# A transfer of turned attention weights issued by ScalarE's queue in place of SP's, in every second round

## The chip, the core and the metric

The kernel runs on one core of a Trainium2 chip. Its engines are TensorE (PE in the profile, with PEld for the loading of matrix weights), VectorE (DVE), ScalarE (ACT), GpSimd (POOL) and SyncE (SP). Each works through its own list of instructions in order and waits on semaphores for the others. A DMA is issued by an instruction in such a list: SP's list holds little else, and ScalarE can issue DMAs too, between its computations. The metric is the device time of one launch in microseconds (us), the median of several runs.

## What is computed

The reference is an attention block with a threshold, followed by a two-layer network. All of it is float32.

```python
# q, k, v: (8, 8, 576, 64) = batch, heads, sequence, head size
scores = scale * np.matmul(q, k.transpose(0, 1, 3, 2))
thresh = np.max(scores, axis=-1, keepdims=True) - tau
scores = np.where(scores >= thresh, scores, -1000000000.0)
scores = scores - np.max(scores, axis=-1, keepdims=True)
attn = np.exp(scores)
attn = attn / (np.sum(attn, axis=-1, keepdims=True) + 1e-09)
out = np.matmul(attn, v)
# bridge: (B,H,S,D) -> (B*S, H*D), so x is (4608, 512)
h = x @ w_in                      # (512, 2048)
g = np.where(h > 0.0, h, np.exp(np.minimum(h, 0.0)) - 1.0)
y = g @ w_out                     # (2048, 512)
```

## The kernel before

**Pairs, steps and rounds.** Two heads of one sequence make a pair; there are 32 (`NP`). The 576 queries of a pair are taken in five steps: steps 0 to 3 have 128 queries of each head, and the tail step, which the code calls `NC` (4), has the last 64 queries of both heads. Pairs 0 to 8 are worked in an opening phase whose order is written out as a long list. From pair 9 (`START`) on there is a loop over rounds `pr` = 9 to 33. A round has the scores of its pair, the turned weights and values of earlier pairs, and 28 quarters of the network's matrix products, which are worked with a fast matrix scheme of seven products (the functions `first_product` and `second_round`, whose matmuls are recorded under line 825).

**One round on TensorE.** First come the scores of steps 0 and 1 (`wide_step(pr, 0)`, line 867), then the scores of the tail step together with the values of pair `pr - 2` (`tail_step`, lines 963, 966 and 974), then 14 quarters, then the scores of steps 2 and 3 (`wide_step(pr, 1)`, line 867 again) and 14 more quarters. A round takes about 33.5 us.

**Scores.** `wide_scores` writes the scores of two steps and two heads, four blocks of 576 columns, into one PSUM tile of six banks of 512 columns each, in eight pieces. After the piece that begins head 1's block of the second step, ScalarE copies one column of it into a small tile called `seen` (line 870). The function `on_banks` keeps a list of the accesses to each PSUM bank and makes an instruction wait for other engines' accesses to its banks. The blocks lie thus that `seen` reads column 1216, and the last piece of the call for steps 2 and 3 writes columns 1024 to 1216. VectorE then takes the row maxima (line 874), ScalarE the exponentials (887), VectorE the mask with the sums (891), and the weights are divided by their sums.

**Turning.** The values need the attention weights transposed. VectorE transposes them in squares of 32 (`turn_squares`, lines 695 and 708); four DMAs then send the squares to a place in DRAM called `there` (line 729, or line 714 for the tail step), and one DMA fetches them back with the squares in their right places (`fetch`, line 740; line 744, with two DMAs, for the tail step). What is fetched lands in the tiles `wTa` (steps 0 and 1) and `wTb` (steps 2 and 3 and the tail). From round 9 on the tail step's transposed squares of pair `pr` are first written to the place in `wTb` that step 3 of pair `pr - 1` will be fetched into, and the sends of line 714 read them there. Round `pr` fetches all five parts of pair `pr - 1`, and round `pr + 1` uses them at line 963.

**The order around the fetch.** The order of every engine's instructions is fixed when the kernel is built. A clock of estimated times runs along TensorE's work; an agenda holds the other engines' work under due times, each with an offset from tables (`MOVED`, keyed `f` for odd rounds and `s` for even ones, and `FIRST` for single rounds); what is due by then is emitted before the next piece of TensorE's work. The five fetches of a round have the due times 9.0, 12.5, 16.0, 20.0 and 24.0 us into it. For the last of them, step 3's, the table has

```python
"ffetch3": -5.52, ... "sfetch3": -3.76,
```

and in odd rounds step 2's fetch has +0.22, so step 3's comes first there. The costs that the clock adds in a round are 2.15 for a wide step, 1.2 + 2.2 + 1.8 for the tail step and 0.87 for each quarter (`QT`).

**SP's queue.** Before the change SP issues everything in the rounds: the sends and fetches of turned weights, the loads of q, k and v (lines 380, 394, 396), of sums of the network's weights (`sw`, line 1168, and `t`, line 1196), and the stores. ScalarE issues three DMAs at the start of the kernel and four stores at its end. Each DMA tells of its landing on a semaphore; these semaphores are few and are used in turn, over both queues, in the order in which the DMAs were emitted.

Of the kernel before, what the change touches and what calls it, by code (L numbers as in the profile page):

```python
# [216 lines left out]
def kernel(  # L217
# [10 lines left out]
    nc = tc.nc  # L228
# [139 lines left out]
    def load(pr, parts=("qm", "km", "v"), shared=False, queue=nc.sync, pieces=tuple((i, d) for i in range(2) for d in range(2)),  # L368
             js=slice(0, S // T)):
        b, j = divmod(pr, NPAIR)  # L370
        tiles = raws.setdefault(pr, {})
        for name, src in (("qm", q), ("km", k)):
            if name not in parts:
                continue
            if name not in tiles:
                tiles[name] = raw.tile([P, S // T, T], FP32, name="qm" if shared else name)
            m = tiles[name]
            for i, d in pieces:
                r = (2 * i + d) * T
                queue.dma_start(  # L380
                    m[r : r + T, js],
                    src[b, 2 * j + i].rearrange("(j t) d -> t j d", t=T)[:, js, d * T : (d + 1) * T],
                )
        if "v" in parts:
            load_v(pr, queue)
# [226 lines left out]
    def turned_tile(pr, i):  # L612
        part = int(i >= 2)
        if pr < NPAIR and i < 2:
            if (pr, "block", i) not in wTs:
                wide_one = (pr + i * NPAIR) % 2
                wTs[pr, "block", i] = wtp.tile([P, (2 + wide_one) * NT, NCH, T], FP32, name="wTb" if wide_one else "wTa")[:, :NT]
            return wTs[pr, "block", i], 0
        if (pr, part) not in wTs:
            wide_one = part  # L620
            wTs[pr, part] = wtp.tile([P, (2 + bool(wide_one)) * NT, NCH, T], FP32, name="wTb" if wide_one else "wTa")[:, : (2 + part) * NT]
        return wTs[pr, part], i % 2 * NT + (NT // 2 if part else 0)
# [112 lines left out]
    def fetch(pr, i, queue=nc.sync):  # L735
        back = turns.pop((pr, i)).rearrange("c k p n -> (c k) p n")
        fetched.add((pr, i))
        wT, g0 = turned_tile(pr, i)
        if i < NC:
            queue.dma_start(wT[:, g0 : g0 + NT].rearrange("p g c n -> p g (c n)"), back)  # L740
        elif pr >= JOINED:
            for h in range(2):
                g = h * (3 * NT - 2)
                queue.dma_start(
                    wT[:, g : g + 2, h * NC : h * NC + NC + 1].rearrange("p g c n -> p g (c n)"),
                    back[:, 2 * h : 2 * h + 2],
                )
        else:
            queue.dma_start(
                wT.rearrange("p (a b) c n -> p a b (c n)", b=2)[:, ::5],  # L750
                back.rearrange("k (a b) n -> k a b n", b=2),
            )
# [453 lines left out]
    def half_sums_x(g, rooms, j, engine=nc.vector):  # L1206
        (b11, b12), (b21, b22) = ([xts[g][:, k + j, t : t + CT] for t in (0, CT)] for k in (0, 2))
        xs = [x[:, j] for x in rooms]
        tt = engine.tensor_tensor
        return [lambda: tt(xs[0], b11, b22, ALU.add), lambda: tt(xs[1], b11, b12, ALU.add), lambda: tt(b12, b12, b22, ALU.subtract),  # L1210
                lambda: tt(xs[2], b21, b22, ALU.add), lambda: tt(b21, b21, b11, ALU.subtract)]
# [341 lines left out]
    with tc.manual_schedule():  # L1553
# [8 lines left out]
        def at(t, f, key=None):  # L1562
            if key and stage[0]:
                t += MOVED.get(stage[0] + key, 0.0)
                t += FIRST.get(f"{stage[3]}:{key}", 0.0)
            elif key:
                t += FIRST.get(f"e:{key}", 0.0)
            serial[0] += 1
            heapq.heappush(agenda, (t, serial[0], f))
# [244 lines left out]
        def group(g):  # L1814
            for r in range(2):
                for u in range(RU * r, RU * r + RU):
                    queue.append((first_product, (g, u)))
                queue.append((second_round, (g, r)))
# [66 lines left out]
        def wide_step(pr, half):  # L1885
            while pr > START and not {("q", pr), ("k", pr)} <= prepared:
                do_next()
            t = clock[0]
            on_pe(2.15, lambda: wide_scores(pr, half, seen_too=not half))
            e = t + 2.15  # L1890
            for s in range(2):
                i = 2 * half + s
                at(e + BOUNDS[half][s], lambda i=i: wide_bounds(pr, i), f"bound{i}")
                for h in range(2):
                    when = PLANS[half][s, h]
                    at(e + when[0], lambda i=i, h=h: wide_max(pr, i, h), f"max{i}{h}")
                    at(e + when[1], lambda i=i, h=h: wide_exp(pr, i, h), f"exp{i}{h}")
                    at(e + when[2], lambda i=i, h=h: wide_mask(pr, i, h), f"mask{i}{h}")
                finish_of(pr, i, e + SUMS[half][s], e + TURNS[half][s])
# [55 lines left out]
        for pr in range(START, NP + 2):  # L1955
            t = clock[0]
            b = pr // NPAIR
            stage[:] = "sf"[pr % 2], 0, 0, pr
            if pr == START + 1:
                ges.append((raw.tile([P, S // T, T], FP32, name="km").rearrange("p j d -> p (j d)")[:, : 2 * CT], lambda: None))  # L1960
            if pr == START:
                for x in range(3):
                    at(t + 18.0 + 6.0 * x, lambda x=x: nc.sync.dma_start(wout_sums[0, x], out_sums[x].rearrange("p u n -> p (u n)")))
            if pr <= NP:
                for i, when in ((NC, 9.0), (0, 12.5), (1, 16.0), (2, 20.0), (3, 24.0)):
                    at(t + when, lambda pr=pr, i=i: fetch(pr - 1, i), f"fetch{i}")
            if pr < NP:
                at(t + 9.0, lambda pr=pr: load(pr, ("v",)))
            if pr < NP:
                wide_step(pr, 0)  # L1970
            tail_step(pr)
            v_end = clock[0]
            if pr % NPAIR == 0 and pr > START:
                in_sums["x", b - 1] = [late["x"].tile([P, 2, CT], FP32, name=f"x{x}") for x in range(3)]
                jobs = half_sums_x(b - 1, in_sums["x", b - 1], 0)
                for x, when in ((1, 5.0), (0, 6.0), (2, 11.0), (3, 15.0), (4, 17.0)):
                    at(v_end + when, jobs[x], f"xsum{x}")
            if pr % NPAIR == 1:
                if b > 1:
                    if ("x", b - 1) in in_sums:  # L1980
                        jobs = half_sums_x(b - 1, in_sums["x", b - 1], 1)
                        for x, when in ((1, -5.0), (0, -0.6), (2, 0.1), (3, 0.5), (4, 1.0)):
                            at(v_end + when, jobs[x], f"ysum{x}")
                    else:
                        jobs = sums_x(b - 1, [late["x"].tile([P, 2, CT], FP32, name=f"x{x}") for x in range(3)])
                        for x, when in ((1, -3.0), (0, -0.6), (2, 0.3), (3, 1.0), (4, 1.8)):
                            at(v_end + when, jobs[x], f"xsum{x}")
                if pr < NP + 1:
                    group(b - 1)
            if pr == NP + 1:  # L1990
                break
            extras(t + 0.6, t + 2.8, t + 6.0, t + 8.0, t + 11.0, t + 14.0, t + 17.0)
            next_q(pr)
            ffn_quarters(HALF_QUARTERS)
            if pr < NP:
                e = clock[0] + 2.15
                wide_step(pr, 1)
                next_k(pr)
                extras(e + 0.3, e + 1.2, e + 4.2, e + 10.4, e + 12.0)
                ffn_quarters(HALF_QUARTERS)  # L2000
            else:
                extras(clock[0] + 0.6)
                ffn_quarters(5)
                while not all((NP - 1, i) in turns_done for i in range(NB)):
                    do_next()
                for r in range(2):
                    for m in DEEP:
                        if PRODUCTS[m][1][0] == "w" and (r, m) not in WHOLE:
                            weigh(r, m)
                for x in range(14):  # L2010
                    at(clock[0] + 0.56 * x + 0.1, lambda: bundles.popleft()(), f"w{x}")
                ffn_quarters(HALF_QUARTERS - 5)
# [332 lines left out]
```

## Time and profile before

| | |
|---|---|
| median of 3 runs | 1247.09 us (1246.99 to 1248.81) |
| the profiled execution | 1250.28 us |
| its span, first to last instruction | 1248.5 us |
| TensorE busy | 1232.1 us, 99% |
| VectorE busy | 1065.3 us, 85% |
| GpSimd busy | 800.9 us, 64% |
| ScalarE busy | 582.5 us, 47% |
| DMA queue of SP (q1) | 275.57 MB, 79.3% of 16 engines' span |
| DMA queue of ScalarE (q10) | 0.69 MB, 0.2% |
| issues of step 2's and 3's fetches (wTb at line 740) | 58, median 6.5 us to landing |

How the rows are read: a timeline row has the start in us from the span's start, the duration in us, the engine, the line of the kernel, the operation, the tile written and the tile read, and how many instructions the row takes together; in brackets stands the engine's idle time before it and what ended it. A `q` behind the engine's name marks its queue: the instruction issues or waits, and is not counted as busy. A row of waits has who waited for whom, then the sum in us, the number of times and the longest. The chain of waits through the profiled execution is on TensorE for 76% of the span.

### The profile page before, as it was taken

The page shows a single profiled execution, that of the slowest core. Times are in us where ns is not written, and L with a number is a line of the kernel's source. Part 1 is how long each engine was busy: PE and PEld are TensorE (multiplying, and loading weights), DVE is VectorE, ACT ScalarE, POOL GpSimd, SP SyncE. Part 2 cuts the span into 40 slices and gives each one's busy share as a digit, 9 for nine tenths or more (in the row PEclk, how much of TensorE's full clock was granted, in tenths as well). Part 3 has the DMA queues.
Part 4 walks back from the last instruction along what each step waited for, and adds up shares of the span by engine and source line. Part 5 has one row for each costly group of instructions (what it writes and reads, how often), then busy time and mean ns, then how long its engine had stood idle before and what let it go on. Part 6 is the DMA issues. An engine that isn't in the chain of part 4 may idle for free.

```text
span 1248.5 us, 32325 instructions
## 1 busy us (share of the span) xinstructions
PE 1232.1 (99%) x12020; PEld 832.1 (67%) x12020; DVE 1065.3 (85%) x2357; ACT 582.5 (47%) x1295; POOL 800.9 (64%) x1151
## 2 busy tenths in 40 slices
PE   8999999999999999999999999999999999999998
PEld 6776575566666666666666666666666666678887
DVE  6998989888899889988898889988998886777877
ACT  7987755453534445353525353444535350434130
POOL 5776644786576848583867657675858383675564
PEclk9999999999999999999999999999999999999999
DMA  9568999899989889898989888898889876444433
GB/s 222 150 185 243 235 251 269 240 275 243 247 215 273 225 259 222 251 252 243 243 231 262 226 267 219 245 238 252 220 257 251 233 223 231 165 136 153 140 110 118
DMA packets 332942, 278.33 MB, mean 223 GB/s; under 512 B 201328, under 2 KB 288368, under 8 KB 332784
## 3 DMA queue, kind: packets, MB, share of 16 engines
q1 hardware_dynamic: 331264, 275.57, 79.3%
q8 instruction: 95, 1.56, 0.5%
q10 hardware_dynamic: 1520, 0.69, 0.2%
q14 instruction: 63, 0.52, 0.1%
HBM read 178.85 MB, written 97.32 MB: 221 GB/s over the span
## 4 chain that ended last, share of the span: by engine, by line
PE 76%; DVE 4%; DMA 3%; SPq 1%; issue 1%; ACT 1%; POOL 1%; DVEq 0%; ACTq 0%
PE f L825 45%; PE sc L825 13%; PE sc L867 7%; PE f L974 7%; PE f L963 1%; DMA there<-x 1%; DVE mx L874 1%; DVE x L695 1%; PE sc L974 1%; DMA wTb<-there 1%; DVE e L891 1%; DVE w_one L891 0%; SPq L380 0%; DMA qm<-in_k_dram 0%; DMA wTa<-there 0%
## 5 line engine op out<-in xcount | busy, mean ns | idle before, releaser
L874 DVE TENSOR_REDUCE mx<-sc 128x1 f32<-128x576 f32 x252 | 180.2, 745 | 13.3 <-PE sc L867 4.8
L887 ACT ACTIVATE w_one<-sc,mx 128x576 f32<-128x576 f32 x140 | 102.9, 741 | 111.1 <-DVE wTb L708 44.3
L883 POOL TENSOR_SCALAR th<-mx,ntau 128x2 f32<-128x2 f32 (+1 forms) x139 | 56.9, 411 | 150.7 <-DVE mx L874 144.6
L891 DVE SCALAR_TENSOR_TENSOR w_one<-sc,th,w_one 128x576 f32<-128x576 f32 x140 | 111.4, 810 | 23.9 <-POOL e L544 9.9
L867 PE MATMUL sc<-kT,qT 64*64 64x320 f32 (+5 forms) x1792 | 121.6, 409 | 1.7 <-DVE w_one L891 1.7
L887 ACT ACTIVATE e<-sc,mx 128x576 f32<-128x576 f32 x112 | 82.3, 745 | 69.6 <-DVE mx L874 64.4
L544 POOL TENSOR_SCALAR w_one<-w_one,rs 128x576 f32<-128x576 f32 x115 | 92.7, 812 | 30.1 <-DVE rs L601 30.1
L867 PEld LDWEIGHTS sc<-kT,qT 64*64 64x64 f32 x1792 | 79.3, 132 | 47.5 <-issue 15.2
L825 PE MATMUL f<-w_out_sb,s 128*64 128x256 f32 (+1 forms) x896 | 105.6, 376 | 0.0
L825 PE MATMUL f<-x,w_in_sb 128*64 128x256 f32 x832 | 101.0, 379 | 0.0
L891 DVE SCALAR_TENSOR_TENSOR e<-sc,th,e 128x576 f32<-128x576 f32 x112 | 87.5, 807 | 8.1 <-ACT e L887 6.9
L825 PE MATMUL f<-t,s 128*64 128x256 f32 (+1 forms) x800 | 93.5, 375 | 0.0
L825 PE MATMUL f<-xt,sw 128*64 128x256 f32 x736 | 91.2, 381 | 1.1 <-DVE g L1638 0.6
L825 PE MATMUL f<-xt,w_in_sb 128*64 128x256 f32 x736 | 90.5, 379 | 0.0
L695 DVE STREAM_TRANSPOSE x<-e 128x640 f32<-128x640 f32 x108 | 77.5, 756 | 14.5 <-POOL e L544 12.4
L544 POOL TENSOR_SCALAR e<-e,rs 128x576 f32<-128x576 f32 x92 | 68.2, 748 | 31.3 <-DVE rs L601 30.0
L695 DVE STREAM_TRANSPOSE x<-w_one 128x512 f32<-128x512 f32 (+1 forms) x117 | 83.3, 749 | 5.6 <-DMA there<-x 2.6
L825 PEld LDWEIGHTS f<-w_out_sb,s 128*64 128x64 f32 x896 | 63.7, 137 | 31.5 <-issue 3.2
L870 ACT COPY seen<-sc 128x1 f32<-128x1 f32 x79 | 12.6, 159 | 154.0 <-PE sc L867 154.0
L825 PEld LDWEIGHTS f<-x,w_in_sb 128*64 128x64 f32 x832 | 61.5, 137 | 28.4 <-ACT g L1677 0.3
L825 PEld LDWEIGHTS f<-t,s 128*64 128x64 f32 x800 | 57.1, 137 | 28.0
L1703 POOL TENSOR_TENSOR s<-g 128x256 f32<-128x256 f32 x96 | 71.0, 742 | 1.9 <-DVE g L1666 1.9
(392 smaller groups left out, 3006.7 us busy)
## 6 DMA issues: line engine op xcount, KB each, us to landing
there<-x SPq DMA_DIRECT2D x452, 144.0 KB, 3.8
wTb<-there SPq DMA_DIRECT2D x58, 576.0 KB, 6.5
wTa<-there SPq DMA_DIRECT2D x55, 576.0 KB, 5.2
sw<-win_sums SPq DMA_DIRECT2D x62, 384.0 KB, 4.9
t<-wout_sums SPq DMA_DIRECT2D x45, 512.0 KB, 4.8
wTb<-there SPq DMA_DIRECT2D x56, 160.0 KB, 2.8
wst<-in_moe_w_in_dram SPq DMA_DIRECT2D x16, 512.0 KB, 4.3
vm<-in_v_dram SPq DMA_DIRECT2D x64, 128.0 KB, 2.8
```

Source lines behind the costliest of these rows:

```text
L544: nc.gpsimd.tensor_scalar(wv, wv, st["rs"][:, h : h + 1], 1.0, ALU.mult, ALU.mult)
L695: nc.vector.transpose(x[:, :, c0 : c0 + nc_], src.rearrange("p (c g n) -> p g c n", c=nc_, n=T))
L825: (note or beside)(nc.tensor.matmul(oy, left[:, y : y + D] if n > D else left, right, skip_group_check=True, **how), oy)
L867: on_banks(nc.tensor.matmul(oy, qT[r, i * P + y * D : i * P + (y + 1) * D], kT[r, k0 : k0 + n], start=True, stop=True, skip_group_check=Tr ...
L870: on_banks(nc.scalar.copy(seen, o[:, :1]), o[:, :1], kept=False)
L874: on_banks(nc.vector.tensor_reduce(st["mx"][:, h : h + 1], st["sc", h], axis=AX.XY if len(st["sc", h].shape) > 2 else AX.X, op=ALU.max, ne ...
L883: nc.gpsimd.tensor_scalar(st["th"][:, cs], st["mx"][:, cs], -1.0, ntau, ALU.mult, ALU.add)
L887: on_banks(nc.scalar.activation(st["e", h], st["sc", h], AF.Exp, bias=st["mx"][:, h : h + 1]), st["sc", h])
L891: on_banks(nc.vector.scalar_tensor_tensor(st["e", h], st["sc", h], st["th"][:, h : h + 1], st["e", h], ALU.is_ge, ALU.mult, accum_out=st[" ...
L963: watch(nc.tensor.matmul(o, vd[r, r], parts[x][r, g0:g1, NC], start=True, stop=False, skip_group_check=True), o)
L974: watch(nc.tensor.matmul(o, vm[:, h, c], parts[part][:, g0:g1, h * (NC + 1) + c], start=False, stop=(c == NC - 1), skip_group_check=True), o)
L1703: engine.tensor_tensor(o, x, y, op)
```

## The change

In the rounds `pr` = 9, 11, ..., 31 the fetch of step 3 of pair `pr - 1` is issued by ScalarE, on its own DMA queue; in the even rounds, and for the other four parts, SP issues as before. The due time, and with it the place of the fetch in the order in which the kernel emits its instructions, stays. The transfer, its source and its destination stay.

```diff
             if pr <= NP:
                 for i, when in ((NC, 9.0), (0, 12.5), (1, 16.0), (2, 20.0), (3, 24.0)):
-                    at(t + when, lambda pr=pr, i=i: fetch(pr - 1, i), f"fetch{i}")
+                    at(t + when, lambda pr=pr, i=i: fetch(pr - 1, i, nc.scalar if i == 3 and pr % 2 else nc.sync), f"fetch{i}")
```

`fetch` had the parameter for the queue already; in the opening phase it is called with it as well.

## The prediction

> **What bounds the kernel now.** I read the page's table of busy time, then the list of TensorE's waits, then the timelines of SP, ScalarE and TensorE around one of the fetches that move.
>
> ```profile
> span 1248.5 us, 32325 instructions
> PE 1232.1 (99%) x12020; PEld 832.1 (67%) x12020; DVE 1065.3 (85%) x2357; ACT 582.5 (47%) x1295; POOL 800.9 (64%) x1151
> PEclk9999999999999999999999999999999999999999
> ```
> ```profile
> PE f L963 <- DMA wTb<-there: 1.2, 1, 1.2
> ...
> PE f L963 <- issue: 0.6, 1, 0.6
> ...
> PE f L963 <- DVE g L1666: 0.4, 1, 0.4
> ```
>
> TensorE is the bound: 1232.1 of 1248.5 us, at the full granted clock. A gain must come out of its few waits, and a pause forced on it is added whole, for nothing else can run in its place. The three waits quoted stand at the start of rounds 18, 22 and 26, where line 963 needs the turned weights of the round before: 2.2 us in all. So no other transfer of turned weights is late, and nothing here can give back more than about 2 us.
>
> **The change part by part.** It hits rounds 9, 11, ... 31, twelve issues. I take round 15, whose fetch of the fourth step is the issue at 472.87. SP's timeline:
>
> ```profile
> 461.97 1.82 SPq L714 DMA_DIRECT2D there<-wTb  x4
> 463.83 0.43 SPq L740 DMA_DIRECT2D wTa<-there  x1
> 464.31 2.39 SPq L380 DMA_DIRECT2D qm<-in_k_dram  x4
> 466.79 2.68 SPq L1168 DMA_DIRECT2D sw<-win_sums  x1
> 469.57 3.25 SPq L729 DMA_DIRECT2D there<-x  x4
> 472.87 0.44 SPq L740 DMA_DIRECT2D wTb<-there  x1
> ```
>
> ScalarE's in the same stretch:
>
> ```profile
> 466.04 0.37 ACT L1678 COPY g<-f 128x256 f32<-128x256 f32 x1 [0.49 <-PE f L825]
> 468.70 0.16 ACT L870 COPY seen<-sc 128x1 f32<-128x1 f32 x1 [2.29 <-PE sc L867]
> ...
> 470.94 0.37 ACT L1630 COPY w<-f 128x256 f32<-128x256 f32 x1 [0.36 <-PE f L825]
> ```
>
> *Where it stands on ScalarE.* By the agenda the fetch is emitted 18.48 us into an odd round (24.0 with the -5.52 of its table entry); the second wide step comes at 2.15 + 5.2 + 14 x 0.87 = 19.53. So on ScalarE's queue the issue stands after the copy of line 1678 (done at 466.41) and ahead of the small copy into seen (468.70). ScalarE would meet it 2.3 us before seen is due, and 4 us before SP, which is in arrears here, gets to it (472.87).
>
> *What it will wait for.* The older DMAs show that an issue waits for another landing than those of its data:
>
> ```profile
> 436.25 1.24 SPq L740 DMA_DIRECT2D wTb<-there  x2
> 437.53 2.55 SPq L729 DMA_DIRECT2D there<-x  x4
> 440.12 5.67 SPq L380 DMA_DIRECT2D qm<-in_q_dram  x4
> ```
> ```profile
> SPq L380 <- DMA wTb<-there: 2.7, 2, 1.5
> ```
>
> The third and fourth load of line 380, which share no tile with the two fetches, waited 2.7 us for these to land. Each stands eight issues behind the fetch it waited for (fetch, fetch, four sends, two loads, load). Completion semaphores are taken in turn, eight of them, and an issue waits until the DMA eight before it has landed; the records of ScalarE's four issues at the very end use the same eight. In round 15 the eight before the fetch are four sends, one load of sums and three loads of k, so it hangs on the second load of line 380:
>
> ```profile
> 464.79 0.50 SPq L380 DMA_DIRECT2D qm<-in_k_dram  x1
> DMA to landing us min/median/max: 5.5/5.5/5.5
> ```
>
> That lands at 464.79 + 5.5 = 470.29, which is 1.59 us after seen now starts. On SP this costs nothing: SP comes to the fetch at 472.87. ScalarE would sit in front of it.
>
> *Who waits behind it.* Behind the issue stand seen, the exponentials and the copies out of PSUM. The nearest is seen. It reads column 1216 of the wide PSUM tile; the last piece of the same scores (192 columns) writes columns 1024 to 1216; both lie in one bank of 512, and the code makes TensorE wait for the other engines' accesses to a bank. TensorE's rows:
>
> ```profile
> 467.65 2.17 PE L867 MATMUL sc<-kT,qT 64*64 64x448 f32 x32
> ```
> ```profile
> 469.32 0.51 PE L867 MATMUL sc<-kT,qT 64*64 64x192 f32 x6
> ```
> ```profile
> L867 PEld LDWEIGHTS sc<-kT,qT 64*64 64x64 f32 x1792 | 79.3, 132 | 47.5 <-issue 15.2
> ```
>
> Seen ends at 468.86 and the last piece starts at 469.32: 0.46 us between, less its weight load of 0.13. The slack is between 0 and 0.33 us; I take 0.2, the middle. What seen is late beyond that, TensorE stands still, with the products of line 825 behind it. The copies of line 1630 are then late by 0.2 us only, measured against TensorE.
>
> *Price of the issue itself.* On SP and on ScalarE:
>
> ```profile
> L740 SPq DMA_DIRECT2D wTb<-there x58: 319/466/1168, 77.9 to 1031.6; - x58
> ```
> ```profile
> L1286 ACTq DMA_DIRECT2D w_out_sb<-in_k_dram x2: 444/592/739, 0.7 to 1.8; - x2
> ```
>
> I take 0.47, the median of the same transfer (0.32 to 1.17 as ends, with ScalarE's 0.74 inside), and 0.05 for the step to the next instruction, as between SP's issues. A pause of TensorE is then (landing of the DMA eight before) - (start of seen) + 0.47 + 0.05 - 0.2, that is the difference + 0.32.
>
> *The sum.* The same reading in every odd round, issue + landing against seen. The first and the last of eleven:
>
> ```profile
> 262.69 0.44 SPq L740 DMA_DIRECT2D wTa<-there  x1
> DMA to landing us min/median/max: 4.9/4.9/4.9
> 938.74 0.32 SPq L380 DMA_DIRECT2D qm<-in_k_dram  x1
> DMA to landing us min/median/max: 5.7/5.7/5.7
> ```
> ```profile
> 267.54 0.16 ACT L870 COPY seen<-sc 128x1 f32<-128x1 f32 x1 [2.29 <-PE sc L867]
> ...
> 941.15 0.16 ACT L870 COPY seen<-sc 128x1 f32<-128x1 f32 x1 [2.29 <-PE sc L867]
> ```
>
> Round 9: 267.59 - 267.54 = 0.05. Round 29: 944.44 - 941.15 = 3.29. Between them, rounds 11 to 27: 4.22, 2.07, 1.59, 4.44, 1.64, 3.00, 1.32, 3.81, 1.97. Round 31 has no loads of k in the queue, and its eighth DMA has landed before ScalarE arrives: 0. The eleven sum to 27.4, and 11 x 0.32 = 3.5 makes 30.9 us of pauses. Against it stand the 2.2 us of line 963: rounds 17, 21 and 25, which end in those waits, are among the longest pauses, so the late weights gain more time than they miss. SP saves 12 x 0.47 = 5.6 us of issuing and the fetch goes out some 2 us sooner; neither is on TensorE's path, so they count as 0 (bounds 0 to the 2.2 just counted). The DMAs themselves move the same bytes. Sum: 30.9 - 2.2 = 28.7 us.
>
> The profiled execution took 1250.28 us (1248.5 of span and 1.8 around it), 3.2 above the median of 1247.09. 1250.28 + 28.7 = 1279.0; against the median 1275.8.
>
> What could shrink it: the sends of line 714 start 6.7 us ahead of seen in round 15 (468.70 - 461.97), and so in most odd rounds, but 5.2 ahead in round 17 (535.76 - 530.53, rows below) and 6.4, 6.2 and 5.9 in rounds 21, 25 and 29. If that is VectorE's arrears, which a pause lets it work off, 1.5 + 0.3 + 0.5 + 0.8 = 3.1 us go; slack of 0.33 takes 1.4 more, an issue of 0.32 another 1.7. What could swell it: ScalarE's 0.74 for 0.47 adds 3.0, no slack adds 2.2, 1.17 adds 7.7.
>
> **The rivals.**
> 1. *Only the data's own landings hold the issue* (no wait for the DMA eight before on ScalarE's queue). Then the last send of line 714 decides:
>
> ```profile
> 530.53 2.29 SPq L714 DMA_DIRECT2D there<-wTb  x4
> ...
> 531.70 1.12 SPq L714 DMA_DIRECT2D there<-wTb  x2
> DMA to landing us min/median/max: 5.3/5.4/5.6
> ```
> ```profile
> 535.76 0.16 ACT L870 COPY seen<-sc 128x1 f32<-128x1 f32 x1 [2.29 <-PE sc L867]
> ```
> In round 17 the last of them, issued at about 532.0, lands at about 537.6, against seen at 535.76: 1.9 + 0.32 = 2.2; read likewise, rounds 21, 25 and 29 give 0.9, 1.4, 0.6, the others 0. 5.1 - 2.2 = +2.9: 1250.0. Against it: SP's 2.7 us wait above. 5%.
> 2. *The issue is covered* (the other side): ScalarE's idle time before seen takes all of it and the three waits of line 963 go, 1247.09 - 2.2 = 1244.9. It decides where the landing comes 0.3 us or more before seen. Rounds 9 and 31 are near that, ten are 1.3 to 4.4 us past it. With the three waits left as they are it is no change, 1247.1. 3% for both. [...]
> 3. *Seen is no gate*: then the copy of line 1630 is, which ends at 471.31 and had 0.36 us of idle time before it.
>
> ```profile
> 472.40 0.82 PE L825 MATMUL f<-xt,w_in_sb 128*64 128x256 f32 x6
> ```
> The products that overwrite its bank start 1.1 us later and pile up behind the earlier ones to 1.2; slack 1.6 in all. The difference + 0.52 - 1.6 leaves 16.6 us over ten rounds, less 2.2: 1261.5. The code's bank rule speaks against it. 7%.
> 4. *TensorE's clock falls after the long pauses.* The trace shows 0.9 or more throughout, but its longest pause after the start is 1.2 us. Rounds 11, 17, 25 and 29 get 4.5, 4.8, 4.1 and 3.6; if each cost half its own length again, 8.5 us: 1284.3. 10%. [...]
>
> **How the numbers follow.** My forecast, eleven pauses with 1275.8 us, has 75%; the rivals have the 25% above. The range 1261 to 1285 takes in the third and fourth rival and the sizes of the issue and the slack except 1.17; it leaves out the first two. About 0.2%, 2.5 us, is what can be told from no change: faster 2% (part of the covered case), same 4% (the rest of it and part of the first rival), slower 94%.
>
> **What would show it.** After: in eleven odd rounds ScalarE's last copy of line 1678 is followed by an issue of line 740, and seen starts about 0.5 us after the eighth DMA before landed; TensorE shows pauses of 0.4 to 4.8 us inside line 867, put down to ScalarE, none in even rounds; the waits of line 963 for wTb are gone; SP's 58 such issues are 46. Wrong would be: seen on time, pauses at line 825 in place of 867, or a clock below 1 behind the pauses.

## The result, and the profile after

The changed kernel takes 1253.83 us (median of ten runs, 1250.2 to 1263.63), the kernel before, timed beside it, 1246.6 us (1245.49 to 1248.81). The ratio is 1.0062, 95% interval 1.0045 to 1.0079: slower by 7.2 us, where the prediction had 1275.8 and nothing under 1261. The profiled execution of the changed kernel took 1250.97 us and is thus one of the shorter ones of its kernel, as the one of before, at 1250.28, is longer than any of the ten. The two profiles stand nearer to each other than the medians do.

From the page of the changed kernel, and from its list of TensorE's waits:

```profile
span 1249.2 us, 32353 instructions
PE 1232.3 (99%) x12020; PEld 830.5 (66%) x12020; DVE 1066.5 (85%) x2357; ACT 581.6 (47%) x1295; POOL 801.3 (64%) x1151
PEclk9999999999999999999999999999999999999999
q10 hardware_dynamic: 3248, 7.77, 2.2%
```
```profile
PE sc L825 <- DVE su L595: 2.6, 3, 1.0
...
PE f L825 <- DMA sw<-win_sums: 0.7, 1, 0.7
...
PE sc L867 <- ACT seen L870: 0.3, 1, 0.3
```

TensorE's work and clock are what they were. The three waits at line 963 are gone. In their place stand four waits at line 825 (the first two rows above), which the prediction did not have, and one short wait at line 867 for `seen`, which it expected eleven times. ScalarE's queue (q10) carries twelve transfers more.

*How the fetch goes now.* Round 15 again, the round that the prediction worked out. ScalarE's timeline, then the groups of line 714 (the sends of the tail step) and of line 380 (the loads of k) in that round, with their time to landing, and the same for ScalarE's fetch:

```profile
464.23 0.37 ACT L1678 COPY g<-f 128x256 f32<-128x256 f32 x1 [0.49 <-PE f L825]
464.69 0.33 ACTq L740 DMA_DIRECT2D wTb<-there  x1
466.89 0.16 ACT L870 COPY seen<-sc 128x1 f32<-128x1 f32 x1 [2.29 <-PE sc L867]
```
```profile
L714 SPq DMA_DIRECT2D there<-wTb x4: 318/451/499, 460.1 to 461.5; - x4
...
DMA to landing us min/median/max: 3.0/3.4/3.7
```
```profile
L380 SPq DMA_DIRECT2D qm<-in_k_dram x4: 317/466/563, 462.5 to 464.4; - x4
...
DMA to landing us min/median/max: 6.5/6.8/7.1
```
```profile
L740 ACTq DMA_DIRECT2D wTb<-there x1: 327/327/327, 464.7 to 464.7; - x1
...
DMA to landing us min/median/max: 7.7/7.7/7.7
```

No load of k has landed before 462.5 + 6.5 = 469.0, and the issue starts at 464.69. So it does not wait for them. It starts as soon as the sends of line 714 have landed, and `seen` runs on time, 1.05 us after the first product of the scores, as before.

SP's row of line 729 in the same round shows where the semaphore's turn went:

```profile
472.38 2.94 SPq L729 DMA_DIRECT2D there<-x  x6
```

That is the third to the eighth send. The third starts at 472.38; ScalarE's fetch lands at 464.69 + 7.7 = 472.39. Fetch, four loads of k, one load of sums, two sends, third send: it stands eight behind the fetch. The rule of eight holds, but the fetch has its turn ahead of the loads of k, not behind the sends where SP used to issue it. The part ahead of the prediction says that the turns go by the order in which the DMAs are emitted, and that this order stays with the due time. The due time is the same here and the turn is not, so the due time does not set the turn. SP's waits at line 729 for such a fetch were 0.8 us in two waits before; after:

```profile
SPq L729 <- DMA wTb<-there: 34.1, 13, 4.7
```

*Where TensorE's new pauses come from.* The group of line 481, VectorE's transposition of k: busy time and mean, then the idle time ahead of it. First of before, then of after:

```profile
L481 DVE STREAM_TRANSPOSE kT<-qm 128x576 f32<-128x576 f32 x21 | 16.1, 766 | 1.7 <-DMA qm<-in_k_dram 1.6
```
```profile
L481 DVE STREAM_TRANSPOSE kT<-qm 128x576 f32<-128x576 f32 x21 | 16.2, 770 | 7.7 <-DMA qm<-in_k_dram 7.7
```

VectorE waits 6 us more for loads of k. Round 27 shows one such wait. Before (SP's timeline, the landing of the four loads, TensorE's scores and VectorE's timeline):

```profile
869.67 2.07 SPq L380 DMA_DIRECT2D qm<-in_k_dram  x4
```
```profile
DMA to landing us min/median/max: 5.3/5.7/6.2
```
```profile
873.04 2.17 PE L867 MATMUL sc<-kT,qT 64*64 64x448 f32 x32
```
```profile
878.39 0.77 DVE L481 STREAM_TRANSPOSE kT<-qm 128x576 f32<-128x576 f32 x1
```

After (the same, with ScalarE's issue):

```profile
868.88 3.32 SPq L380 DMA_DIRECT2D qm<-in_k_dram  x4
```
```profile
DMA to landing us min/median/max: 6.1/6.6/8.3
```
```profile
870.95 0.33 ACTq L740 DMA_DIRECT2D wTb<-there  x1
```
```profile
878.94 0.78 DVE L481 STREAM_TRANSPOSE kT<-qm 128x576 f32<-128x576 f32 x1 [1.24 <-DMA qm<-in_k_dram]
```
```profile
872.27 2.17 PE L867 MATMUL sc<-kT,qT 64*64 64x448 f32 x32
...
882.22 1.08 PE L825 MATMUL sc<-xt,sw 128*64 128x256 f32 x8 [0.72 <-DVE su L595]
```

The fetch now travels at the same time as the loads of k, and these take 6.1 to 8.3 us to land where they took 5.3 to 6.2. The transposition stands at a fixed place in VectorE's list; it now starts 6.67 us after the scores (878.94 - 872.27), and 5.35 before (878.39 - 873.04). Behind it in the list come the masks of line 891 and the addition of line 1638 that gives TensorE its PSUM bank back:

```profile
881.75 0.42 DVE L1638 TENSOR_TENSOR g<-sc,t 128x256 f32<-128x256 f32 x1
```

It ends at 882.17, and TensorE's product of line 825 starts 0.05 us later, ten us after the scores. (TensorE's row names line 595, a short sum that VectorE runs just behind.) Counted from the scores the addition starts 1.1 us later than before, where it started at 881.43.

Over the rounds 11, 13, ... 29, from the start of the second scores: the issue of the last load of k ends at 0.42 us before and at 0.48 after, nearly the same; it lands at 4.20 and at 6.06. The issue of the fetch ends at 5.72 and at 0.33. The third send of line 729 starts at 3.85 and at 6.20, after the change in each of these rounds some 0.02 us behind the landing of the fetch.

*The wait at* `seen`, round 25, ScalarE's and TensorE's timelines:

```profile
806.24 0.35 ACTq L740 DMA_DIRECT2D wTb<-there  x1
806.63 0.16 ACT L870 COPY seen<-sc 128x1 f32<-128x1 f32 x1 [3.49 <-DMA wTa<-there]
```
```profile
806.84 0.54 PE L867 MATMUL sc<-kT,qT 64*64 64x192 f32 x4 [0.29 <-ACT seen L870]
```

Here the last send of line 714 lands late and holds the issue; `seen` starts 2.25 us after the scores in place of 1.05.

*The balance of the two profiles.* From the first scores of round 9 to the last scores the execution of before took 762.05 us, that of after 764.51. Without any pause but the one in round 9 that all share, this stretch takes 758.2 (the run kearly_sp, below). So before had 3.9 us of pauses there (the waits of line 963 among them) and after has 6.3: 1.3 of them in rounds 17, 21 and 25, by how late `seen` was less the slack that the run kearly shows below, and nearly all the rest at line 825 in six odd rounds. Before had about 1 us at line 825 too, in rounds 17 and 29. Outside the stretch it is the other way round, 1250.28 - 762.05 = 488.2 us before and 1250.97 - 764.51 = 486.5 after, which is why the two profiles stand so near to each other.

### The profile page after: what moved, and what is told of

It is laid out like the page before. It is cut to its first block, busy times and chain, and to the rows that moved or that the text cites. A ratio compares the mean times of both kernels' runs of the same rounds, so it can differ in the third digit from the quotient of the medians.

```text
span 1249.2 us, 32353 instructions
## 1 busy us (share of the span) xinstructions
PE 1232.3 (99%) x12020; PEld 830.5 (66%) x12020; DVE 1066.5 (85%) x2357; ACT 581.6 (47%) x1295; POOL 801.3 (64%) x1151
## 4 chain that ended last, share of the span: by engine, by line
PE 83%; DMA 6%; DVE 4%; SPq 3%; ACT 2%; issue 1%; POOL 0%; DVEq 0%; ACTq 0%
PE f L825 43%; PE sc L825 12%; PE sc L867 8%; PE f L974 7%; DMA qm<-in_k_dram 2%; DMA wTa<-there 2%; PE sc L1102 2%; PE f L1061 1%; PE f L963 1%; PE sc L536 1%; PE f L1102 1%; PE sc L768 1%; DMA wTb<-there 1%; PE f L1033 1%; PE f L604 1%
## 5 line engine op out<-in xcount | busy, mean ns | idle before, releaser
L825 PEld LDWEIGHTS f<-xt,sw 128*64 128x64 f32 x736 | 52.6, 137 | 29.6 <-DVE g L1638 3.3
```

Source lines behind the costliest of these rows:

```text
L825: (note or beside)(nc.tensor.matmul(oy, left[:, y : y + D] if n > D else left, right, skip_group_check=True, **how), oy)
```

## The experiments

Three theories. **A**: ScalarE's issue holds the copy into `seen`, and TensorE's last piece of scores waits. **B**: the fetch, sent out beside the loads of k, makes these land later, line 481 waits, and TensorE pauses at line 825. **C**: the semaphore's turn makes SP stand at the third send of line 729 until the fetch has landed, and what SP issues after it is late. Ratios are to the kernel before, timed beside each, with 95% intervals.

| run | us | ratio | last load of k lands, us after the scores | idle before line 481, us |
|---|---|---|---|---|
| before | 1246.2 to 1247.2 | 1 | 4.20 | 1.7 |
| after | 1253.83 | 1.0062 [1.0045, 1.0079] | 6.06 | 7.7 |
| again | 1253.88 | 1.0063 [1.0046, 1.008] | 6.05 | 8.0 |
| late | 1269.03 | 1.016 [1.0132, 1.0187] | 4.47 | 4.3 |
| kearly | 1263.0 | 1.0121 [1.0104, 1.0139] | -1.04 | 0.0 |
| kearly_sp | 1245.34 | 0.999 [0.9978, 1.0002] | -1.07 | 0.0 |
| past | 1255.54 | 1.0071 [1.0056, 1.0087] | 5.59 | 6.9 |
| sp_early | 1257.92 | 1.0087 [1.0064, 1.0109] | 7.20 | 19.6 |
| past_kearly | 1255.7 | 1.0079 [1.0058, 1.0099] | -0.58 | 0.3 |
| late_two | 1254.32 | 1.0058 [1.0036, 1.008] | 4.56 | 2.7 |
| split | 1250.94 | 1.0033 [1.002, 1.0046] | 5.66 | 3.5 |
| after_two | 1258.72 | 1.0091 [1.0077, 1.0105] | 6.21 | 10.0 |
| eight | 1249.05 | 1.0016 [1.0005, 1.0026] | 5.55 | 5.4 |
| kearly_sp2 | 1246.1 | 0.9991 [0.9982, 1.0] | -1.36 | 0.0 |

The fourth column is the mean over rounds 11, 13, ... 29 of when the last load of line 380 lands, from the first product of the round's second scores; the fifth is the group of line 481 on `qm` in each profile. Both come from one profiled execution of each run, and those of late (1273.71 us) and sp_early (1265.64) were the longest of their runs. The times of before are the medians beside the four sets of runs.

### The change once more: again

No edit.

> The changed kernel once more, for a second profile. Theory A (the wait): ScalarE's issue holds the copy into seen where the last send of line 714 lands late, in rounds 17, 21, 25 and 29; pauses in line 867 of 0.2 to 0.9 us there and nothing else new. Theory B (the transfer): the fetch goes out 6 to 9 us earlier, beside the loads of k, these land 5.3 to 7 us after the start of the second scores in place of 2.7 to 6.3, and VectorE's transposition of k (line 481) waits for them; pauses of 0.3 to 1.3 us at line 825 some 9 us after those scores, in most odd rounds. Time by either: 1251 to 1257 us.

1253.88 us, and the same two kinds of pauses: `seen` is late in rounds 13, 17, 25 and 29 (by 0.1, 1.4, 1.1 and 0.4 us), line 481 waits 8.0 us. This profiled execution took 1253.53 us, its stretch from round 9 on 765.23, so 7.1 us of pauses. Which odd rounds pause differs between the two executions; that they do, and where in the round, does not.

### The fetch 5.5 us later: late

```diff
-                    at(t + when, lambda pr=pr, i=i: fetch(pr - 1, i, nc.scalar if i == 3 and pr % 2 else nc.sync), f"fetch{i}")
+                    at(t + when + (5.5 if i == 3 and pr % 2 else 0.0), lambda pr=pr, i=i: fetch(pr - 1, i, nc.scalar if i == 3 and pr % 2 else nc.sync), f"fetch{i}")
```

> ScalarE still issues the fetch in the odd rounds, but 5.5 us later in the agenda, behind its copy into u in place of ahead of seen, about when SP issued it. By A and by B alike the loss goes: seen on time, loads of k landed 2.7 to 6.3 us after the start of the second scores. Time 1244 to 1248 us. If the loss came from ScalarE's issuing as such (its price, its own DMA queue), it stays: 1251 to 1257 us.

1269.03 us: a miss for both theories, though each saw its own step come out. `seen` is on time in every round, and the loads of k land at 4.47. Instead:

```profile
SPq L729 <- DMA wTb<-there: 64.7, 13, 7.7
```
```profile
L963 PE MATMUL f<-wTb,vd 64*64 64x320 f32 x92 | 17.0, 438 | 15.2 <-DVE mx L874 4.2 <-DMA sw<-win_sums 3.7 <-issue 2.8
```

SP's wait at the third send has doubled. The fetch's turn stayed where it was although the fetch was put 5.5 us further back; the third send starts at 8.96 us after the scores, 0.02 after the fetch's landing, and step 2's fetch, which SP issues behind the sends, goes out at 11 to 14 us and in most of these rounds lands after line 963 of the next round needs it. From this came theory C.

These waits are longer than any in the profiles before, and the clock shows them. Stretches around the start of rounds 24 and 14: from and to, length, TensorE's busy time, granted clock, share of the DMA engines, GB/s:

```profile
765.06:768.47 3.41, 1.63 (x24) 1.00 1.23 207
768.47:771.88 3.41, 3.41 (x16) 0.50 0.97 280
771.88:775.30 3.42, 3.42 (x34) 1.00 0.76 209
420.31:423.72 3.41, 1.70 (x28) 1.00 1.14 178
423.72:427.13 3.41, 3.41 (x35) 1.00 0.76 205
```

Soon behind a wait of 1.78 us the clock is 0.50 for 3.41 us, which costs half of that, 1.7 us more. The same follows the waits of 2.66 and 2.03 us in this run, and not those of 1.61, 1.71 (the last two rows) and 1.92 us. The last part of this document sets these waits beside those of the other runs.

### Step 2's fetch ahead of the sends: late_two

To the kernel of late one edit is added, in the table of offsets:

```diff
... (the table, cut to the entry that changes)
-"ffetch2": 0.22
+"ffetch2": -3.60
```

> The kernel of the run late (ScalarE's fetch 5.5 us later in the agenda, 1269 us) with one more edit: the fetch of the third step of odd rounds 3.82 us earlier, so that SP issues it ahead of the sends of line 729 and not behind the third one, which stands until ScalarE's fetch has landed. Theory C: the pauses at line 963 vanish and the time falls below 1255 us, to 1246 to 1254. If something other than SP's stand at the third send made those pauses, it stays at 1264 to 1272 us.

1254.32 us, 14.7 less than late and 0.3 above the range for C. The waits of line 963 are gone but for one of 0.7 us, so what made them was step 2's fetch held behind SP's stand: theory C holds in late. (The stand itself is still there, 63.4 us.) It is no return to 1247. Step 2's fetch now stands ahead of a load of sums, ScalarE's is issued beside it, and TensorE waits for that load:

```profile
PE f L825 <- DMA sw<-win_sums: 3.6, 3, 3.2
```

The one of 3.2 us, in round 13, is followed by 3.41 us at a clock of 0.50 again, and the round is 5.1 us late.

### The loads of k earlier, with and without the change: kearly, kearly_sp, kearly_sp2

The same edit to the changed kernel (kearly) and to the kernel before (kearly_sp, repeated as kearly_sp2):

```diff
... (the table, cut to the entry that changes)
-"floadk": 2.18
+"floadk": -3.50
```

> The changed kernel with the loads of k of the odd rounds moved 5.68 us earlier in the agenda, ahead of the first wTa fetch and so ahead of the moved fetch. B: line 481 waits no more, its pauses go, what is left is the pauses at seen; 1247 to 1250 us. A: the pauses at seen are the loss and stay, or grow, since line 714's sends now stand behind the loads; 1251 to 1258 us.

> The kernel before with the same earlier loads of k: the base for the run above. Line 481 hardly waits in the kernel before, so both theories expect no more than the pause of round 29 (0.8 us) to go: 1244 to 1249 us.

> The kernel before with only the loads of k 5.68 us earlier in the agenda, every fetch on SP: the run kearly_sp once more, since it stood at 0.999 of the kernel before, too near to be told apart. If the pauses that before has in its loop (2.2 us at line 963 and 1 us in the odd rounds 17 and 29) are what it saves: 1244 to 1245 us, ratio 0.998. If it is no gain: 1246 to 1248 us.

On SP the edit leaves no pause in the stretch of rounds but round 9's, 758.18 us in both executions; 1245.34 and 1246.1 us, 0.1% below before, which is less than can be told from no change. If the edit does nothing else, the median execution of before has about 1 us of pauses (2.7 at most by the wider interval), and not the 3.9 of its profiled one.

With the fetch on ScalarE it is 1263.0, above A's range too. Line 481 waits no more, so nothing is left of B. But the sends of line 714 now stand behind the loads, land later, and hold ScalarE's issue longer. TensorE's waits, and ScalarE in round 17:

```profile
PE sc L867 <- ACT seen L870: 9.0, 7, 2.2
```
```profile
540.38 0.36 ACTq L740 DMA_DIRECT2D wTb<-there  x1
540.77 0.16 ACT L870 COPY seen<-sc 128x1 f32<-128x1 f32 x1 [5.38 <-DMA sw<-win_sums]
```

So A is real, and the pair of runs prices it where the landing is late: 17.7 us. It also gives the slack. Where `seen` was late by 1.85, 0.94 and 1.76 us (rounds 13, 15, 27), the next scores came 1.49, 0.57 and 1.39 late: a slack of 0.36 or 0.37 each time. Round 17 lost 4.41 for 3.09 - 0.37 = 2.7, with a clock of 0.50 for 3.41 us behind its wait.

### The fetch behind `seen`: past

```diff
-                    at(t + when, lambda pr=pr, i=i: fetch(pr - 1, i, nc.scalar if i == 3 and pr % 2 else nc.sync), f"fetch{i}")
+                    at(t + when + (1.1 if i == 3 and pr % 2 else 0.0), lambda pr=pr, i=i: fetch(pr - 1, i, nc.scalar if i == 3 and pr % 2 else nc.sync), f"fetch{i}")
```

> ScalarE's fetch of the odd rounds is emitted 1.1 us later, so that it stands right behind the copy into seen instead of ahead of it; nothing else is moved. Theory A (the issue holds the copy into seen): no pause at line 867, and if that were the whole of the loss, 1246 to 1248 us. Theory B (the fetch travels beside the loads of k, whose transposition in line 481 then waits): the fetch goes out some 2 us later than in the changed kernel but still ahead of where SP issued it, so pauses of 0.3 to 1 us at line 825, some ten us behind the scores, stay in several odd rounds: 1250 to 1254 us. Theory C (the third send of line 729 takes its semaphore after the fetch and SP stands until the fetch has landed): that wait grows by the same 2 us, and pauses at line 963 begin to come back: 1252 to 1258 us.

1255.54 us, no better than the change, with `seen` on time in every round: A at `seen` is not needed for a loss of this size. The time is above B's range and inside C's, but no wait at line 963 comes back, which is what C had. TensorE's waits:

```profile
PE sc L825 <- DVE su L595: 2.7, 2, 1.4
PE f L825 <- DMA sw<-win_sums: 2.5, 3, 0.9
```

The loads of k still land at 5.59. Both rows go back to loads that SP has under way while ScalarE's fetch travels, of k and of the sums. The fetch goes out at 1.86 us in place of 0.33, and the third send starts at 6.80. Round 17 alone is 4.4 us late: its two waits, 0.95 and 1.35 us, are followed by a clock of 0.50 for 3.41 us. A new pause of 0.7 us stands in round 10, where the loads of k land late behind SP's stand in round 9; that it is C's is likely, and no run here shows it.

### Both at once: past_kearly

The edits of past and of kearly together.

> The changed kernel with two edits: the loads of k 5.68 us earlier in the agenda, and ScalarE's fetch right behind the copy into seen. Neither A nor B can act: seen is ahead of the issue, and k has landed before the fetch goes out. Theories A and B together as the whole of the loss: 1244 to 1247 us, as the kernel before with the loads of k so moved (1245.3). Theory C: the third send of line 729 still waits for the fetch, which now goes out later, and step 3's fetch lands late for line 963: 1248 to 1256 us.

1255.7 us: a miss for A and B. The number lies in C's range, but no wait at line 963 shows. With `seen` ahead of the issue, the next copy behind it is the gate. TensorE's wait, and ScalarE in round 21:

```profile
PE f L825 <- ACT w L1630: 4.8, 3, 2.2
```
```profile
672.11 0.16 ACT L870 COPY seen<-sc 128x1 f32<-128x1 f32 x1 [2.29 <-PE sc L867]
675.65 0.33 ACTq L740 DMA_DIRECT2D wTb<-there  x1
```

The issue stands 3.4 us for the last send of line 714, and the copy of line 1630 that gives a bank back is late. It is theory A at the next instruction: whatever stands behind the issue on ScalarE waits for that landing.

### SP issues early itself: sp_early

To the kernel before:

```diff
... (the table, cut to the entry that changes)
-"ffetch3": -5.52
+"ffetch3": -9.10
```

> The kernel before, every fetch on SP, but the fetch of the fourth step of odd rounds is moved 3.6 us ahead in the agenda, so that SP itself issues it right behind the second fetch into wTa and ahead of the loads of k. ScalarE issues nothing. Theory A: with no issue on ScalarE there is no loss, 1246 to 1248 us. Theory B: the loads of k land later than before by 1 to 3 us, line 481 waits for them, and pauses at line 825 appear without any at line 867: 1250 to 1260 us (SP also stands at the fetch until the sends of line 714 have landed, up to 1 us, which makes the loads later still). Theory C alone: SP's sends wait for the fetch as in the changed kernel, 1247 to 1250 us.

1257.92 us without any issue on ScalarE, inside B's range. Line 481 waits 19.6 us, and TensorE's waits are

```profile
PE sc L825 <- DVE su L595: 8.4, 7, 1.5
PE f L825 <- DMA sw<-win_sums: 4.3, 4, 1.5
```

That loads of k which land late make just these pauses is shown. The reason of the lateness is another than in the change, though: SP stands at the fetch until the sends have landed, and the last load's issue ends at 3.24 us in place of 0.42, while its landing takes 3.97 us from there (before 3.78, after 5.58). So the loads that followed the fetch on one queue took little longer than before (3.97 us for 3.78), and the loads beside it on another queue took 5.58. The two runs differ in the moment as well: here the last load goes out 2.5 us behind the fetch, in the change 0.15. Which of the two matters, the queue or the moment, they do not separate.

### Half the bytes: split

```diff
-            queue.dma_start(wT[:, g0 : g0 + NT].rearrange("p g c n -> p g (c n)"), back)
+            half = NT // 2 if queue is nc.scalar and pr >= START - 1 else NT
+            queue.dma_start(wT[:, g0 : g0 + half].rearrange("p g c n -> p g (c n)"), back[:, :half])
+            if half < NT:
+                nc.sync.dma_start(wT[:, g0 + half : g0 + NT].rearrange("p g c n -> p g (c n)"), back[:, half:])
```

The lines behind it are numbered 3 higher, so that 870 is the scores' and 873 the line of `seen`.

> The changed kernel, but ScalarE fetches only the first half of the turned weights of that step (288 KB) at its new place, and SP the second half at the old place, behind the sends of line 729. Everything is fetched. Theory A (the issue holds seen): the issue stands where it stood, so the pauses at line 867 in rounds 17, 21, 25 stay and the time is that of the changed kernel, 1252 to 1255 us. Theory B (the bytes beside the loads of k): the last load of k, which landed 4.2 us after the start of the second scores before and 6.1 after, lands at about 5.1, just ahead of the slot of line 481 at 5.35, and most pauses at line 825 go: 1247 to 1251 us. Theory C (third send): it stands until the half has landed, about 1 us sooner than in the changed kernel; no pause follows from it either way.

1250.94 us, inside B's range and below A's. The wait of line 481 is 3.5 us, less than half of what the whole fetch makes. Two of TensorE's pauses are those of `seen`:

```profile
PE sc L870 <- ACT seen L873: 3.3, 2, 1.8
```

The loads land at 5.66, later than the 5.1 expected. In this execution A cost more than B (rounds 17 and 21 lost 4.5 us of 6.1, most of it at `seen`).

### Two fetches beside the loads: after_two

The edit of late_two, made to the changed kernel.

> The changed kernel with one edit: the fetch of the third step of odd rounds 3.82 us earlier, so that SP issues it ahead of the sends of line 729 and it no longer waits behind the third send. ScalarE's fetch stays where the change put it. Theory C as a part of the loss: 1248 to 1252 us. Theory B: the loads of k now share the way with two fetches instead of one, so line 481 is as late or later and the pauses at line 825 stay or grow: 1253 to 1260 us. Theory A: seen is as late as in the changed kernel, 1253 to 1255 us.

1258.72 us, inside B's range. With step 2's fetch out of C's reach nothing is won; but a second fetch now travels beside the loads, so C is not taken out alone. `seen` is late by up to 1.05 us, line 481 waits 10.0 us, and TensorE waits for the load of sums that stands behind the loads of k:

```profile
PE f L825 <- DMA sw<-win_sums: 8.5, 8, 1.8
```

### Eight of the twelve rounds: eight

```diff
-                    at(t + when, lambda pr=pr, i=i: fetch(pr - 1, i, nc.scalar if i == 3 and pr % 2 else nc.sync), f"fetch{i}")
+                    at(t + when, lambda pr=pr, i=i: fetch(pr - 1, i, nc.scalar if i == 3 and pr in (9, 11, 13, 15, 19, 23, 27, 31) else nc.sync), f"fetch{i}")
```

> The changed kernel with ScalarE's fetch in rounds 9, 11, 13, 15, 19, 23, 27 and 31 alone; rounds 17, 21, 25 and 29, the ones in which seen was late, keep it on SP. Theory A: no pause at line 867, and the three waits at line 963 (2.2 us) stay as before: 1247 us, no difference. Theory B: the loads of k land late in six of these rounds, with pauses at line 825 of 0.1 to 1.2 us each: 1248.5 to 1251 us. If the loss were the same in every round that moves, 8/12 of 7 us: 1251.5 us.

1249.05 us, 2 above before and inside B's range, with 5.4 us of waiting ahead of line 481. The pauses are at line 825 in rounds 11, 13 and 19 and, as before, 29; none is at line 963, and one of 0.3 us is at `seen`. By this run the four rounds left out hold some 5 of the 7 us, where A and B act in the same round.

This run has its own comparison for B, within one execution (of 1252.0 us). In the six rounds from 11 on with ScalarE's fetch the last load of k took 5.90 us from the end of its issue to its landing, in the four without it 3.98. Before, the same rounds had 3.72 and 3.87.

### What the runs say together

The loss is made in the odd rounds by two effects of one transfer: B in most of them, A in those where the sends of line 714 land late. None of the places tried on ScalarE takes them out: ahead of `seen` the issue holds `seen`; with the loads of k moved out of the fetch's way the sends come late, and it holds `seen` longer or, behind `seen`, the copy of line 1630. C costs some 15 us where the fetch is later still (late against late_two). In the change itself none of TensorE's listed waits goes back to it, but no run takes C out alone. What stays open: the exact share of A and B in the 7.2 us, since the rounds that pause differ from one execution to the next; how many pauses a median execution of before has, since its one profiled execution is 3.7 us above that median; and whether the queue or only the moment of the fetch makes the loads late.

## Why the prediction was wrong

*That it is slower, and by what means TensorE can lose time*: right. TensorE is the bound, busy for 1232.3 of 1249.2 us; I added each pause whole. But the forecast was of waits at `seen` in eleven rounds, and in the profile of after `seen` costs time in three; that the sign came out is due in the main to another cause.

*"What it will wait for"*: this is the step that failed. The rule read from SP's 2.7 us wait, that an issue waits for the DMA eight before it, holds; SP's third send shows it in the odd rounds from 11 to 29, where it starts some 0.02 us behind the landing of the fetch eight ahead of it. But I counted the eight along SP's list of before. On ScalarE the fetch takes its turn ahead of the loads of k, with the same due time, and it keeps that turn in late and past, where it is due 5.5 and 1.1 us later. The DMA eight before it, in round 15 a fetch of line 744, had landed long before (by 457.1 + 2.8 = 459.9, in the rows below), so the 27.4 us of waits for the second load of k were not there.

```profile
L744 SPq DMA_DIRECT2D wTb<-there x2: 467/524/581, 456.5 to 457.1; - x2
...
DMA to landing us min/median/max: 2.6/2.7/2.8
```

*The first rival* had what took its place: the data's own landings hold the issue in rounds 17, 21, 25 and 29. In these `seen` was late by 0.66, 0.58, 1.20 and 0.31 us, and TensorE by 0.3, 0.2, 0.8 and 0; the rival had 2.2, 0.9, 1.4 and 0.6. It was given 5% because SP's wait seemed to speak against it. It did not: both hold, for different landings. Its 1250.0 us is 3.8 below the measured time, mostly by what the next point left out.

*"Neither is on TensorE's path, so they count as 0"*: the second step that failed. The fetch went out not 2 us sooner but 5.4, and to where the loads of k are under way. I had weighed the transfer's bytes, which are the same, and not what travels beside them. In the profile of after, about 5 us of pauses stand at line 825 (6.3 less 1.3; before had about 1), the very sign that the prediction named for being wrong.

*Seen as the gate*: right, with a slack of 0.37 us where I had 0.2 out of 0 to 0.33. *Price of the issue*: 0.33 us, near the lower end of the range; I took 0.47, the median of SP's. ScalarE's twelve vary little, in the row below. *The waits of line 963*: gone, as said, but for another reason in two of three rounds. They were for step 2's fetch, which in rounds 21 and 25 landed 16.80 and 17.59 us after the second scores and now lands at 14.06 and 15.50. In round 17 it is later, 17.71 for 17.20, and there TensorE's own pause of 1.3 us covers it but for 0.2. *SP's issues*: 58 became 46, as said, and brought nothing.

```profile
L740 ACTq DMA_DIRECT2D wTb<-there x12: 326/327/357, 263.3 to 1007.3; - x12
```
```profile
L740 SPq DMA_DIRECT2D wTb<-there x46: 319/454/1526, 77.3 to 1032.2; - x46
```

*The clock*: no pause of the changed kernel's profile lowered it (1.00 throughout the span); the longest in the rounds is 1.0 us, the longest of all, in the opening phase, 1.6. The fall that the fourth rival supposed is seen in other runs: late, late_two and kearly have it after single waits of 1.8 to 3.2 us, past after two shorter ones. No run shows the rival's term, half a pause's own length again; what they show is 3.41 us at 0.50, some 1.7 us more, behind a wait of 1.78 us (late) as behind one of 3.2 (late_two). Whether a fall came in among the unprofiled executions is open. One of the ten had a mean granted clock of 0.996 (1256.81 us); 0.998 and 0.999, which four others had, occur before the change as well, in executions of 1245.1 to 1250.3 us.

## What to carry to other kernels

Moving a DMA to another engine's queue changed three things here beside who pays for the issue: which landing its own issue hangs on (that of the sends of line 714), which later DMA of the old queue now hangs on its landing (the third send; SP's waits at line 729 for such a fetch went from 0.8 to 34.1 us), and what travels beside it (the last load of k, 5.58 us to its landing for 3.78). Read the semaphores' turns anew from a trace of the changed kernel, for here they followed neither the old list nor the due time, and look for loads under way at its new time that have a reader at a fixed place; that reader's slack, here 1.15 us between 4.20 and 5.35, is the price to compare. ScalarE's idle time ahead of a small copy, 2.29 us, was no free place for a DMA that must wait for data: what stood behind it waited for that data too, and TensorE with it (9.0 us for `seen` in kearly, 4.8 for the copy of line 1630 in past_kearly).

## What the runs showed of the hardware

**Loads of k beside a fetch.** From the end of its issue to its landing the last load of k took 3.78 us before, and 5.58 and 5.27 (after and again) with the 576 KB of the fetch on ScalarE's queue beside it. With half of them (split) it took 5.05, and 3.97 when it followed the whole fetch on SP's own queue (sp_early). By this figure half the bytes is not clearly told from the whole; with the fetch from without it is, most plainly in the run eight, with 5.90 against 3.98. No view shown here follows the single packets, so what makes the landing longer stays open.

**TensorE's clock behind waits.** In the rounds the clock falls to 0.50 behind some waits and not behind others. In late it falls at 768.47, 908.41 and 980.09 us, for 3.41 us each time, behind waits of 1.78, 2.66 and 2.03 us. It falls for 3.41 us behind the wait of 3.2 us in late_two, behind one of 2.2 us in round 17 of kearly, and behind the two waits of 0.95 and 1.35 us in past. In sp_early the 20 us from 810 on have a mean clock of 0.86, with TensorE busy for 17.09 of them. The clock stays at 1.00 behind waits of 1.61, 1.71 and 1.92 us in late, 1.83 in split, 1.98 in kearly and 2.23 in past_kearly. So the length of a single wait does not tell whether the clock falls: it fell behind 1.78 us and not behind 2.23. What else decides it stays open.
